# Expert rows read by a transposing DMA instead of a plain DMA and PE transposes

## The chip, the cores and the metric

The kernel runs on one core of a Trainium2 chip. A core has a matrix engine (PE, with its weight loads listed apart as PEld), a vector engine (DVE), a scalar engine (ACT), a general engine (POOL) and a queue engine (SP) that here only issues DMAs. Each engine works through its own queue in order and waits on semaphores that the others raise. DMAs are issued from the queues of SP and POOL and are moved by the core's 16 DMA engines. On-chip memory is SBUF (128 partitions) and PSUM, into which PE writes. The metric is the device time of one execution in microseconds; less is better.

## The reference

The program is blockwise causal attention followed by a mixture of experts with a noisy top-2 router. Cut to what matters:

```python
# attention: batch 8, 8 heads, 576 positions, head size 64; masked by blocks of 64 positions
attn = softmax(scale * q @ k.T, mask) @ v
x = attn.transpose(0, 2, 1, 3).reshape(4608, 512)        # N tokens, D = 512

# router: two experts of eight for each token
noisy = x @ w_gate + log1p(exp(x @ w_noise)) * noise
top2, top2_w = two largest of noisy, softmax over these two

# experts: D = 512 -> F = 1024 -> 512
for e in range(8):
    for k in range(2):
        mask = top2[:, k] == e
        h = np.maximum(x[mask] @ w1[e], 0.0)
        out[mask] += top2_w[mask, k, None] * (h @ w2[e])
```

## The kernel before

The kernel works in bfloat16 with accumulation in float32. The 4608 tokens are cut into four groups of two batch entries (g = 0 to 3, nine tiles of 128 tokens each) and two halves (half 0 is groups 0 and 1, half 1 is groups 2 and 3).

**Attention and router, for each group (L202 to L366).** q and k are loaded and transposed on PE, scores go through PE (L233) and ACT's exponential (L237), PE multiplies by v (L261, L275), and DVE normalizes into the tile `xr` (L279), one row of 512 numbers for each token. `xr` has two buffers, so groups 1 and 3 share one. The router transposes `xr` on PE, computes logits (L292), and DVE picks the two experts of each token and its place among the rows of each expert (L301 to L352); the counts come from two small matmuls `pp` (L328, L329). POOL then scatters each row of `xr` with 18 indirect DMAs for each group (L357) into a DRAM bucket, `xd[half]`, in which each expert has CAP = 640 rows.

**Experts, for each half and each of the eight experts (the loop over `seq`, from L430).** Experts are counted 0 to 15 here; 0 to 7 are the eight of half 0. `load_x` (L378) reads the 640 rows of one expert from the bucket into the tile `xg`, five blocks of 128 rows with a row in each partition, by one DMA on SP's queue; it depends on all scatters of that half. `xg` has three buffers, and the program asks for the load of expert i + 2 ahead of the work of expert i. `expert` (L386) then turns the rows into `xgT`, in which the partition is the place in d and the row is along the free axis: for each of four blocks of d, five PE transposes (L392) into one PSUM tile and one copy by DVE (L393). The first layer `hp` (L399) takes 64 matmuls of 128x128 by 320 columns; ACT applies the rectifier into `hsb` (L402), eight times for an expert. The second layer `yp` (L407) takes 40 matmuls of 512 columns, eight to a block of 128 rows; DVE casts each block into `ysb` (L410), and SP stores it to a second DRAM bucket `yd` (L411). `hp` and `yp` have two PSUM buffers each.

**Combine, once for each half (`combine`, L413 to L428).** For each of 18 tiles of tokens POOL gathers the two result rows of each token from `yd` with two indirect DMAs (L419), DVE weights and adds them (L424, L425), and SP stores the output (L428). The combine of half 0 comes in the program after expert 7 and ahead of expert 8, that of half 1 at the end.

**What sets the order.** The queues of the engines are in the order that the framework's scheduler chose when it built the program, which need not be that of the text: loads and transposes stand ahead of work that waits. Dependencies between instructions become semaphore waits. The pools of the expert part (from L368, opened when those of the attention part have closed) take SBUF that the attention part used; the first writer of a tile waits for whoever used that memory last. The pools open in the order weights `wL`, `xgp` (3 buffers of 5,120 B in each partition), `xgtp` (2 of 5,120 B), `hp` (2 of 10,240 B), `yp` (6 of 1,024 B), `fin`.

**Weights.** Those of experts 0 and 1 of each half (the same eight sets serve both halves) are loaded during the last attention group, the others by POOL-issued DMAs after it (L113 to L118, called at L433).

A branch for buckets that overflow (from L452) is compiled in and isn't taken with these inputs.

Of the kernel before, what the change touches and what calls it, by code (L numbers as in the profile page):

```python
# [9 lines left out]
BF16 = mybir.dt.bfloat16  # L10
# [9 lines left out]
def kernel(  # L20
# [12 lines left out]
    nc = tc.nc  # L33

    B, H, S, D = q.shape
    N, Dm = out.shape
# [3 lines left out]
    P = 128  # L40
    DB = Dm // P
# [6 lines left out]
    CAP = 640  # L48
    CT = CAP // P
# [9 lines left out]
    xd = [nc.dram_tensor(f"xd{i}", (XR, Dm), BF16, kind="Internal").ap() for i in range(NH)]  # L59
# [16 lines left out]
    ident = consts.tile([P, P], BF16)  # L76
# [50 lines left out]
    with tc.tile_pool(name="raw", bufs=2) as raw_pool, \  # L127
# [61 lines left out]
        for i in range(NH):  # L189
            zr = OVB // P  # L190
            nc.sync.dma_start(
                out=xd[i][0:OVB, :].rearrange("(p a) d -> p (a d)", p=P).rearrange("p (a c) -> p a c", c=2048),
                in_=zero.unsqueeze(1).to_broadcast([P, zr * Dm // 2048, 2048]))
# [8 lines left out]
        for g in range(NG):  # L202
            half = g // 2
# [15 lines left out]
            for st in range(H // SET):  # L219
# [33 lines left out]
                for idx in range(TG):  # L253
                    av = av_ps.tile([P, SET, D + 1], F32, tag="av")
                    for hh in range(SET):
                        h = st * SET + hh
                        if idx < 8:
                            hf, ib = divmod(idx, 4)
                            for jt in range(ib + 1):
                                c = EO[jt] + (ib - jt) * P  # L260
# [3 lines left out]
                        else:  # L264
                            for jt in range(5):
                                for hf in range(2):
                                    sl = slice(64 * hf, 64 * hf + 64)
                                    if jt < 4:
                                        c = EO[jt] + (4 - jt) * P
# [15 lines left out]
            for idx in range(TG):  # L285
                tp = tr_ps.tile([P, DB, P], BF16, tag="tr")
# [80 lines left out]

    with tc.tile_pool(name="wL", bufs=1) as wL, \  # L368
         tc.tile_pool(name="xgp", bufs=3) as xg_pool, \
         tc.tile_pool(name="xgtp", bufs=2) as xgt_pool, \  # L370
         tc.tile_pool(name="hp", bufs=2) as h_pool, \
         tc.tile_pool(name="yp", bufs=6) as y_pool, \
         tc.tile_pool(name="fin", bufs=4) as fin, \
# [2 lines left out]
         tc.tile_pool(name="ft_ps", bufs=2, space=PSUM) as ft_ps:  # L376

        def load_x(half, e):  # L378
            xg = xg_pool.tile([P, CT, Dm], BF16, tag="xg")
            ins = nc.sync.dma_start(out=xg, in_=xd[half][e * CAP:(e + 1) * CAP, :]  # L380
                                    .rearrange("(c p) d -> p c d", p=P))
            for nm in scat[half]:
                tc.add_manual_dep(ins.ins, nm, SYNC_DEP, reason="rows landed")
            return xg

        def expert(half, e, xg):  # L386
            w1sb, w2sb = wload[e]
            xgT = xgt_pool.tile([P, DB, CAP], BF16, tag="xgT")
            for db in range(DB):
                tp = ft_ps.tile([P, CAP], BF16, tag="ft")  # L390
                for c in range(CT):
                    nc.tensor.transpose(tp[:, c * P:(c + 1) * P], xg[:, c, db * P:(db + 1) * P], ident)  # L392
                nc.vector.tensor_copy(xgT[:, db, :], tp)  # L393
            hsb = h_pool.tile([P, FB, CAP], BF16, tag="hsb")
            for fb in range(FB):
                hp = hp_ps.tile([P, 2, 512], F32, tag="hp")
                for db in range(DB):
                    for n in range(2):
                        nc.tensor.matmul(out=hp[:, n, 0:NW], lhsT=w1sb[:, db, fb * P:(fb + 1) * P],  # L399
                                         rhs=xgT[:, db, n * NW:(n + 1) * NW],  # L400
                                         start=(db == 0), stop=(db == DB - 1))
                nc.scalar.activation(out=hsb[:, fb, :].rearrange("p (n w) -> p n w", n=2),  # L402
                                     in_=hp[:, :, 0:NW], func=AF.Relu)
            for c in range(CT):
                yp = yp_ps.tile([P, Dm], F32, tag="yp")
                for fb in range(FB):
                    nc.tensor.matmul(out=yp, lhsT=hsb[:, fb, c * P:(c + 1) * P], rhs=w2sb[:, fb, :],  # L407
                                     start=(fb == 0), stop=(fb == FB - 1))
                ysb = y_pool.tile([P, Dm], BF16, tag="ysb")
                nc.vector.tensor_copy(ysb, yp)  # L410
                nc.sync.dma_start(out=yd[half][e * CAP + c * P:e * CAP + (c + 1) * P, :], in_=ysb)  # L411
# [120 lines left out]
```

## Time and profile before

| | us |
|---|---|
| median of 3 runs | 726.08 |
| lowest and highest | 724.75 to 729.91 |
| the profiled execution | 728.31 |
| its span (first to last instruction) | 726.50 |
| PE busy in the span | 472.7 |
| DVE busy | 253.3 |
| ACT busy | 187.3 |
| POOL busy | 218.7 |

The profile is one execution, recorded by the hardware. Times are microseconds from the start of the span unless marked ns. A row of the timeline gives the start, the length, the engine, the line of the kernel, the operation, what it writes and reads, the number of instructions merged in the row and, in brackets, how long the engine had been idle before it and what ended that. A row of the chain of waits gives start, length and the work; the chain is followed back from the last instruction to whatever released each step. A group row gives the line, the engine, the operation, the shapes and the count, then busy time and mean ns, then the idle time ahead of it by releaser. In the table of stretches each row has the busy time and the count of instructions of each engine within one stretch, the TensorE clock that was granted as a share of full speed, the share of time for which the DMA engines were busy, and what they moved.

### The profile page before, as it was taken

The page shows a single profiled execution, that of the slowest core. Times are in us where ns is not written, and L with a number is a line of the kernel's source. Part 1 is how long each engine was busy: PE and PEld are TensorE (multiplying, and loading weights), DVE is VectorE, ACT ScalarE, POOL GpSimd, SP SyncE. Part 2 cuts the span into 40 slices and gives each one's busy share as a digit, 9 for nine tenths or more (in the row PEclk, how much of TensorE's full clock was granted, in tenths as well). Part 3 has the DMA queues.
Part 4 walks back from the last instruction along what each step waited for, and adds up shares of the span by engine and source line. Part 5 has one row for each costly group of instructions (what it writes and reads, how often), then busy time and mean ns, then how long its engine had stood idle before and what let it go on. Part 6 is the DMA issues. An engine that isn't in the chain of part 4 may idle for free.

```text
span 726.5 us, 10418 instructions
## 1 busy us (share of the span) xinstructions
PE 472.7 (65%) x4264; PEld 292.6 (40%) x4264; DVE 253.3 (35%) x591; ACT 187.3 (26%) x245; POOL 218.7 (30%) x244
## 2 busy tenths in 40 slices
PE   2087788361786284039999999964179999996000
PEld 1045446130563163025555555541055555553000
DVE  3054946150474155002222222235332222221443
ACT  0084480160415130013322222230033322221000
POOL 5126625777004413370000000077600000001773
PEclk9988866555566566559999999995589999999555
DMA  9999999492001209969942212256432221111564
GB/s 207 343 231 169 181 195 177 142 124 101 1 2 60 73 15 260 210 133 221 226 125 73 71 55 59 72 176 200 150 105 73 73 73 37 37 37 46 177 192 146
DMA packets 102902, 91.62 MB, mean 126 GB/s; under 512 B 49088, under 2 KB 86976, under 8 KB 102848
## 3 DMA queue, kind: packets, MB, share of 16 engines
q0 software_dynamic: 67744, 49.84, 45.8%
q1 hardware_dynamic: 35104, 41.05, 17.7%
q8 instruction: 35, 0.57, 0.3%
q14 instruction: 19, 0.16, 0.1%
HBM read 81.97 MB, written 39.85 MB: 168 GB/s over the span
## 4 chain that ended last, share of the span: by engine, by line
PE 50%; issue 12%; DMA 9%; another core or an unknown queue 9%; POOL 7%; DVE 7%; ACT 6%; POOLq 0%; DVEq 0%; ACTq 0%; SPq 0%
PE hp L399 18%; PE yp L407 18%; ACT esc L237 6%; POOL yg L419 4%; DMA kr<-in_k_dram 4%; PE av L261 4%; DMA vt<-in_v_dram 3%; PE sc L233 2%; PE av L275 2%; POOL xd L357 2%; PE tp L392 2%; PE tp L166 2%; DVE ysb L410 1%; PE tp L288 1%
## 5 line engine op out<-in xcount | busy, mean ns | idle before, releaser
L399 PE MATMUL hp<-xgT,w 128*128 128x320 bf16 x1024 | 149.9, 305 | 33.6 <-ACT hsb L402 33.6
L419 POOL DMA_INDIRECT yg<-yd,gslots x72 | 75.6, 1050 | 317.6 <-PE hp L399 149.4
L402 ACT ACTIVATE hsb<-hp 128x640 bf16<-128x640 f32 x128 | 89.9, 703 | 288.7 <-PE hp L399 246.6
L407 PE MATMUL yp<-w,hsb 128*128 128x512 bf16 x640 | 146.4, 388 | 17.8 <-DVE ysb L410 14.8
L399 PEld LDWEIGHTS <-w 128*128 128x128 bf16 x1024 | 101.5, 100 | 74.8 <-issue 34.0
L410 DVE CAST ysb<-yp 128x512 bf16<-128x512 f32 x80 | 55.3, 691 | 212.3 <-PE yp L407 203.3
L237 ACT ACTIVATE esc<-sc 128x1024 bf16<-128x1024 f32 x96 | 91.5, 1036 | 127.8 <-PE sc L233 72.2
L407 PEld LDWEIGHTS <-hsb 128*128 128x128 bf16 x640 | 63.5, 99 | 94.5 <-issue 24.5
L357 POOL DMA_INDIRECT xd<-xr,slots x72 | 71.0, 986 | 92.8 <-DVE slots L352 46.9
L233 PE MATMUL sc<-qT,kT 64*128 64x512 bf16 (+4 forms) x320 | 52.8, 376 | 29.4 <-ACT esc L237 27.4
L261 PE MATMUL av<-vt,esc 128*128 128x65 bf16 x640 | 42.6, 234 | 38.5 <-DVE xr L279 29.7
L261 PEld LDWEIGHTS <-esc 128*128 128x128 bf16 x640 | 34.4, 123 | 52.9 <-DVE xr L279 35.1
L155 POOL DMA_DIRECT2D vt<-in_v_dram x40 | 33.7, 867 | 53.6 <-DMA kr<-in_k_dram 14.2
L392 PE MATMUL tp<-ident,xg 128*128 128x128 bf16 x320 | 27.7, 233 | 28.5 <-DVE xgT L393 24.6
L393 DVE COPY xgT<-tp 128x640 bf16<-128x640 bf16 x64 | 29.0, 486 | 47.9 <-PE hp L399 44.8
L392 PEld LDWEIGHTS <-xg 128*128 128x128 bf16 x320 | 23.0, 105 | 35.8 <-DVE xgT L393 17.6
L278 DVE RECIPROCAL rden<-av 128x4 f32<-128x4 f32 x72 | 13.0, 182 | 68.1 <-remote 41.7
L166 PE MATMUL tp<-ident,qr 128*64 128x128 bf16 (+1 forms) x320 | 18.8, 274 | 27.2 <-DMA qr<-in_q_dram 14.8
L233 PEld LDWEIGHTS <-kT 64*128 64x128 bf16 x320 | 15.1, 102 | 51.5 <-issue 47.2
L172 DVE COPY qT<-tp 128x1024 bf16<-128x1024 bf16 (+1 forms) x20 | 22.3, 1117 | 33.8 <-PE tp L166 20.3
L425 DVE SCALAR_TENSOR_TENSOR acc<-yg,wts,acc 128x512 f32<-128x512 bf16 x36 | 26.5, 748 | 17.8 <-DMA yg<-yd,gslots 17.7
L424 DVE TENSOR_SCALAR acc<-yg,wts 128x512 f32<-128x512 bf16 x36 | 19.0, 529 | 35.8 <-DMA yg<-yd,gslots 31.1
(78 smaller groups left out, 278.9 us busy)
## 6 DMA issues: line engine op xcount, KB each, us to landing
w<-in_moe_w_dram POOLq DMA_DIRECT2D x16, 1024.0 KB
xd<-zero SPq DMA_DIRECT2D x2, 5120.0 KB
xg<-xd SPq DMA_DIRECT2D x16, 640.0 KB
yd<-ysb SPq DMA_DIRECT2D x80, 128.0 KB
out_dram<-acc SPq DMA_DIRECT2D x32, 256.0 KB
vt<-in_v_dram POOLq DMA_DIRECT2D x32, 128.0 KB
qr<-in_q_dram POOLq DMA_DIRECT2D x8, 384.0 KB
kr<-in_k_dram POOLq DMA_DIRECT2D x8, 384.0 KB
```

The source lines that it names most:

```text
L155: nc.gpsimd.dma_start(out=vb[p0:p0 + n, idx, :, 0:D], in_=v[b, :, s0:s0 + n, :].rearrange("h s d -> s h d"))
L166: nc.tensor.transpose(tp[64 * hf:64 * hf + 64, r * n:(r + 1) * n], raw[p0:p0 + n, src_t, r * 64:(r + 1) * 64], ident[p0:p0 + n, p0:p0 + n])
L233: nc.tensor.matmul(out=sc[:, hf, off:off + z - a], lhsT=kT[sl, c0 + jt * P:c0 + jt * P + P], rhs=qT[sl, c0 + a:c0 + z], start=True, stop=True)
L237: nc.scalar.activation(out=esc[:, hh, :, u * 512:(u + 1) * 512], in_=sc, func=AF.Exp, scale=scale)
L261: nc.tensor.matmul(out=av[:, hh, :], lhsT=esc[:, hh, hf, c:c + P], rhs=vb[:, 4 * hf + jt, h, :], start=(jt == 0), stop=(jt == ib))
L357: ins = nc.gpsimd.indirect_dma_start(out=xd[half], out_offset=bass.IndirectOffsetOnAxis(ap=slots[:, t0 + idx, i:i + 1], axis=0), in_=xr[:, ...
L392: nc.tensor.transpose(tp[:, c * P:(c + 1) * P], xg[:, c, db * P:(db + 1) * P], ident)
L399: nc.tensor.matmul(out=hp[:, n, 0:NW], lhsT=w1sb[:, db, fb * P:(fb + 1) * P], rhs=xgT[:, db, n * NW:(n + 1) * NW], start=(db == 0), stop=( ...
L402: nc.scalar.activation(out=hsb[:, fb, :].rearrange("p (n w) -> p n w", n=2), in_=hp[:, :, 0:NW], func=AF.Relu)
L407: nc.tensor.matmul(out=yp, lhsT=hsb[:, fb, c * P:(c + 1) * P], rhs=w2sb[:, fb, :], start=(fb == 0), stop=(fb == FB - 1))
L410: nc.vector.tensor_copy(ysb, yp)
L419: nc.gpsimd.indirect_dma_start(out=yg[:, i, :], out_offset=None, in_=yd[half], in_offset=bass.IndirectOffsetOnAxis(ap=gslots[:, t, i:i + 1 ...
```

## The change

The load of an expert's rows becomes a DMA that transposes 2-byte elements on its way from the bucket into SBUF, and writes the layout [d, row] that the first layer reads. The tile `xg` keeps its three buffers and its 5,120 B in each partition, with the shape of `xgT`. The transposes on PE, their PSUM tile and the copies by DVE are gone from `expert`, and so is the pool `xgtp`. The `ft` PSUM pool stays, for the overflow branch. The load is issued from the same queue, with the same dependencies on the scatters.

```diff
     with tc.tile_pool(name="wL", bufs=1) as wL, \
          tc.tile_pool(name="xgp", bufs=3) as xg_pool, \
-         tc.tile_pool(name="xgtp", bufs=2) as xgt_pool, \
          tc.tile_pool(name="hp", bufs=2) as h_pool, \
...
         def load_x(half, e):
-            xg = xg_pool.tile([P, CT, Dm], BF16, tag="xg")
-            ins = nc.sync.dma_start(out=xg, in_=xd[half][e * CAP:(e + 1) * CAP, :]
-                                    .rearrange("(c p) d -> p c d", p=P))
+            xg = xg_pool.tile([P, DB, CAP], BF16, tag="xg")
+            ins = nc.sync.dma_start_transpose(out=xg, in_=xd[half][e * CAP:(e + 1) * CAP, 0:Dm])
             for nm in scat[half]:
                 tc.add_manual_dep(ins.ins, nm, SYNC_DEP, reason="rows landed")
             return xg

-        def expert(half, e, xg):
+        def expert(half, e, xgT):
             w1sb, w2sb = wload[e]
-            xgT = xgt_pool.tile([P, DB, CAP], BF16, tag="xgT")
-            for db in range(DB):
-                tp = ft_ps.tile([P, CAP], BF16, tag="ft")
-                for c in range(CT):
-                    nc.tensor.transpose(tp[:, c * P:(c + 1) * P], xg[:, c, db * P:(db + 1) * P], ident)
-                nc.vector.tensor_copy(xgT[:, db, :], tp)
             hsb = h_pool.tile([P, FB, CAP], BF16, tag="hsb")
```

## The prediction

> **What bounds the kernel now.** I read three views: the table of stretches (busy time of each engine from one moment to the next), the chain of waits for the moments at which work ends, and the timeline for what each engine waited on. The stretches come first (columns: stretch, its length, busy us and instructions of PE, PEld, DVE, ACT and POOL, granted PE clock, DMA share, GB/s).
>
> ```profile
> span 726.5 us, 10418 instructions
> core 0: us, PE busy (x) PEld busy (x) DVE busy (x) ACT busy (x) POOL busy (x), PEclk, DMA share, GB/s
> 0.00:269.50 269.50, 157.12 (x2226) 103.66 (x2226) 118.67 (x338) 96.71 (x114) 115.24 (x142) 0.69 0.95 135
> 269.50:319.00 49.50, 11.47 (x122) 8.76 (x123) 11.56 (x45) 0.73 (x4) 22.77 (x24) 0.59 0.84 199
> 319.00:470.00 151.00, 147.12 (x931) 87.58 (x931) 37.21 (x64) 44.87 (x64) 5.06 (x7) 0.98 0.52 116
> 470.00:530.00 60.00, 25.26 (x133) 13.01 (x130) 26.93 (x47) 5.62 (x8) 38.30 (x36) 0.69 0.55 176
> 530.00:667.00 137.00, 131.71 (x858) 79.55 (x858) 36.23 (x64) 39.37 (x56) 0.00 (x0) 0.99 0.17 56
> 667.00:726.50 59.50, 0.00 (x0) 0.00 (x0) 22.66 (x36) 0.00 (x0) 37.28 (x36) 0.53 0.52 162
> ```
>
> Attention runs to 269.5 and the diff does not touch it. In the two stretches of expert work, 319 to 470 and 530 to 667, PE is busy 147.1 of 151 and 131.7 of 137 us at a clock of 0.98 and 0.99: PE sets the pace there. In 269.5 to 319 and 470 to 530 PE works 11.5 and 25.3 us and otherwise waits; there the question is for what. After 667 no PE work is left (the last gathers).
>
> One expert in steady state, from the chain (start, length, what), the timeline and the groups of the page:
>
> ```profile
> 384.13 8.65 PE yp L407 x40
> 392.60 0.72 PE L392 MATMUL tp<-ident,xg 128*128 128x128 bf16 x10
> 393.41 1.92 DVE L393 COPY xgT<-tp 128x640 bf16<-128x640 bf16 x4
> 393.94 0.44 PE L392 MATMUL tp<-ident,xg 128*128 128x128 bf16 x5 [0.62 <-DVE xgT L393]
> 394.80 8.62 PE hp L399 x63
> 403.42 8.65 PE yp L407 x40
> L392 PE MATMUL tp<-ident,xg 128*128 128x128 bf16 x320 | 27.7, 233 | 28.5 <-DVE xgT L393 24.6
> L393 DVE COPY xgT<-tp 128x640 bf16<-128x640 bf16 x64 | 29.0, 486 | 47.9 <-PE hp L399 44.8
> ```
>
> From one second layer (yp) to the next is 403.42 - 384.13 = 19.29 us. Of these 8.62 are hp and 8.65 yp; the other 2.02 us are the twenty transposes of x and PE's wait of 0.62 for the copies out of PSUM.
>
> The two stretches in which PE waits:
>
> ```profile
> 269.72 12.45 SPq L380 DMA_DIRECT2D xg<-xd  x5
> 274.34 1.09 PEld L392 LDWEIGHTS <-xg 128*128 128x128 bf16 x11 [0.70 <-DMA xg<-xd]
> 275.10 0.49 DVE L393 COPY xgT<-tp 128x640 bf16<-128x640 bf16 x1 [0.53 <-PE tp L392]
> 279.44 0.19 PE L328 MATMUL pp<-m,ones_mat 128*128 128x72 bf16 x1
> 280.26 0.48 DVE L393 COPY xgT<-tp 128x640 bf16<-128x640 bf16 x1
> 284.90 0.98 PEld L392 LDWEIGHTS <-xg 128*128 128x128 bf16 x10 [3.29 <-DMA xg<-xd]
> 284.20 1.05 POOL L357 DMA_INDIRECT xd<-xr,slots  x1 [10.62 <-DVE cmax L446]
> 303.54 0.98 POOL L357 DMA_INDIRECT xd<-xr,slots  x1 [4.08 <-DMA w<-in_moe_w_dram]
> 318.97 1.30 ACT L402 ACTIVATE hsb<-hp 128x640 bf16<-128x640 f32 x2 [39.55 <-DMA xd<-xr,slots]
> 319.73 9.60 PE L399 MATMUL hp<-xgT,w 128*128 128x320 bf16 x48 [33.58 <-ACT hsb L402]
> 346.65 8.63 PE yp L407 x40
> 364.84 8.65 PE yp L407 x40
> 461.28 8.65 PE yp L407 x40
> 473.45 1.07 POOL L419 DMA_INDIRECT yg<-yd,gslots  x1 [149.39 <-PE hp L399]
> 510.20 3.47 PE L407 MATMUL yp<-w,hsb 128*128 128x512 bf16 x8 [1.84 <-issue]
> 521.90 1.01 POOL L419 DMA_INDIRECT yg<-yd,gslots  x1 [0.30 <-issue]
> 524.91 0.69 DVE L410 CAST ysb<-yp 128x512 bf16<-128x512 f32 x1 [9.03 <-remote]
> 529.95 0.88 DVE L393 COPY xgT<-tp 128x640 bf16<-128x640 bf16 x2
> 530.49 1.25 PE L392 MATMUL tp<-ident,xg 128*128 128x128 bf16 x10 [16.82 <-DVE xgT L393]
> 531.74 9.83 PE hp L399 x64
> 541.57 8.65 PE yp L407 x40
> 657.30 8.65 PE yp L407 x40
> ```
>
> At the start expert 0's x has landed by 274.34, yet ACT's first write to hsb waits 39.55 us, until 318.97, for the scatter of the last group (xd<-xr). The scatter writes DRAM; hsb waits because it lies where xr lay, and the scatter reads xr until then. In the combine PE is done with expert 8 at 510.20 + 3.47 = 513.67 and idles 16.82 us: expert 9's transposes need PSUM that DVE frees by the xgT copies, and those stand behind the whole combine in DVE's queue (529.95).
>
> **The change, part by part.**
>
> Removed: 320 transposes and weight loads on PE, 64 copies on DVE (27.7 and 29.0 us busy in the groups above). On the path each steady expert loses its 2.02 us and falls to 8.62 + 8.65 = 17.27. The cover under it: ACT needs 0.70 us (44.87 / 64 in the stretch from 319) per hp group of 1.08 and DVE 0.69 (the cast at 524.91) per yp group of 1.73, so neither becomes the bound. Experts 3 to 7 and 10 to 15 give 11 x 2.02 = 22.2 us. Expert 2, half of whose transposes ran early, ends at 364.84 + 8.65 = 373.49, 18.21 after expert 1 (346.65 + 8.63 = 355.28); it gives 0.94. Experts 0 and 1 were transposed before 319: nothing from PE.
>
> Moved: the pool of xgT (two buffers of 4 x 640 x 2 = 5,120 B a partition) goes, so hp, y and fin, opened behind it, lie 10,240 B lower, if pools lie in the order in which they open. One hsb buffer is 8 x 640 x 2 = 10,240 B, exactly the two xgT buffers. So the first hsb comes to lie where xgT lay, and DVE wrote both xgT buffers by 275.10 and 280.26, forty us before the scatter ended. The second hsb takes the place of the first and waits for 318.97 as that did; ysb (6 x 1,024 B) takes the place of the second. Expert 0 can then do all of hp and, with two PSUM banks, two of its five yp groups before 319; the fill of two hp groups of expert 1, which PE did for expert 0 before, stays. From 319.73 on are left 24 yp matmuls (24 x 8.65 / 40 = 5.19), 48 hp of expert 1 (48 x 8.62 / 64 = 6.47), its yp (8.65), and the slow clock after the idle time: the 48 hp after the stall took 9.60 instead of 6.47, so 3.13. Expert 1 ends at 319.73 + 5.19 + 6.47 + 8.65 + 3.13 = 343.17 instead of 355.28: 12.1 us. Bounds: nothing (rival 2) to 15 with a warm clock.
>
> Through expert 7: 343.17 + 6 x 17.27 = 446.79 against 461.28 + 8.65 = 469.93, a gain of 23.1. Weights do not hold it: DMA is busy for 0.52 of the 151 us from 319, 78.5 us; were all of that, and at the front, the weights of experts 4 to 7, they would land at 339, 358, 378 and 397, and these experts now start at 378, 395, 412 and 430.
>
> The combine: DVE passed its end 529.95 - 469.93 = 60.0 us after expert 7, paced by POOL, whose 36 gathers go from 473.45 to 521.90, 48.45 / 35 = 1.38 each. Nothing of that changes, so DVE is through at 446.79 + 60.0 = 506.8. But hp of expert 9 needs no DVE now: PE goes on right after expert 8 (40.2 us after the first gather, so about 490.5) and has hp and two yp groups done by the time DVE is free. Left are one cast (0.69), 24 yp matmuls (5.19) and a cold clock: between 1.2 and 3.1 us (hp of expert 9 took 9.83 in the chain; of expert 0, above); I take 2. Expert 9 ends at 514.7 instead of 541.57 + 8.65 = 550.2: 35.5, of which 12.4 come from this stretch.
>
> ```profile
> L380 SPq DMA_DIRECT2D xg<-xd x16: 360/371/524, 269.7 to 590.8; - x16
> q0 software_dynamic: 67744, 49.84, 45.8%
> ```
>
> Added: sixteen transposing loads on SP instead of plain ones, 655,360 B each. No row shows one. Nearest below: the plain load, from issue at 269.72 to 274.34, 4.6 us. Above: by packets. The software queue's took 0.458 x 726.5 x 16 / 67,744 = 78.6 ns each on an engine; if every 256 B run of a row (one block of 128 elements) is a packet, a load has 2,560, or 12.6 us over 16 engines. I take about 5, near the plain row, since the bytes and the queue are the same. Every load is asked for well ahead: its buffer frees when hp of the expert three before is done, that is 8.6 us later than now, with two experts and more (over 34.5 us) to land in. So both 4.6 and 12.6 cost nothing there.
>
> The Trainium skill speaks against this: "VectorE: DVE Perf Modes", section "The three transpose paths", gives 1309 ns for a 128x128 block by the DMA crossbar, so twenty blocks would be an estimated 26.2 us, and the sum would come out near 766. Its page "DMA: Bandwidth & Descriptors", section "Latency and other measured facts", gives 261 GB/s for a transposing DMA, an estimated 2.5 us, and leaves the sum as it is. No run here shows either; the first of the two is a case of rival 1 and within its chance.
>
> New waits and queues: a load now waits on SP for hp of its buffer's last expert, and behind it stand that expert's five yd stores. If SP is held for the whole load (a plain one holds it 0.37 us) and that is 12.6, the last store of expert 7 leaves 8.6 + 12.6 - 17.3 = 3.9 late and delays the combine by so much; at 5 nothing. POOL's queue keeps its order. PE has the two pp matmuls of the router (279.44) behind the first expert work; if x of expert 0 lands 8 us later, they and the scatter start that much later, but the scatters start at 284.20, one in 1.35, and the eighth was held for weight loads until 303.54, 9.9 us after it could have gone, so that is covered too.
>
> Sum: 23.1 + 12.4 + 6 x 2.02 (experts 10 to 15) = 47.6. The profiled execution took 728.31 (span 726.5 and 1.8 around it), 2.2 above the median of 726.08. From the median: 678.5; I say 679.
>
> **Rivals.**
> Rival 1, slower: the transposing loads set the pace. They run one behind another from 269.72, so the last lands at 269.72 + 16T and its expert ends 17.27 later; before it ended at 657.30 + 8.65 = 665.95. The point that decides is T = 23.7 us. If the load is cut into 128 B pieces, 5,120 packets of 78.6 ns over 16 engines make T = 25.2: end 690, time 750. Against it: three plain loads had landed by 284.90, beside weight loads (DMA share 0.84).
> Rival 2: nothing is pulled ahead of 319 (hsb still waits for the scatter, or PE's order does not let expert 0 through). Then the first half gives 0.94 + 5 x 2.02 = 11.0 instead of 23.1: 691. The place of hsb is worked out, not seen.
> Rival 3: expert 9 does not get ahead, because DVE's queue has the casts of expert 8 too late in the combine (one stood at 524.91 after 9.03 us that no engine explains). Then that stretch gives 2.0 instead of 12.4: 689.
> That T lies near 23.7 and all cancels is the case of no change.
>
> **How the numbers follow.** The forecast 0.66, rival 2 0.12, rival 3 0.12, no change 0.04, rival 1 0.06. A measurement of this kernel tells about 1% from nothing. Faster by more: 0.66 + 0.12 + 0.12 = 0.90; within: 0.04; slower: 0.06. The range goes up to 700 (rivals 2 and 3 together give 25.2: 701) and down to 668 (the 9.03 us stall gone as well, 670, and less lost to a cold clock).
>
> **What would show it.** Right: hp and yp alternate without a gap every 17.3 us; ACT's first hsb write lies before 290; experts 0 and 1 have 112 matmuls left after 319 instead of 192; hp of expert 9 starts before DVE ends the combine; PE no longer waits for xgT. Wrong: PE waiting for DMA xg<-xd (rival 1), a first hsb write still at 319 (rival 2), PE idle between experts 8 and 9 until the combine's end (rival 3), the scatter ending later than 319, or yd stores held back behind a load on SP.

## The result, and the profile after

The changed kernel takes 703.86 us (median of 4 runs, 701.40 to 708.35) against 727.52 (724.75 to 729.91) for the kernel before on the same chip: a ratio of 0.968, with a 95% interval of 0.962 to 0.975. It is faster, by 23.7 us, half of the 47 forecast, and its time lies just above the range of 668 to 700. Its profiled execution took 701.40 with a span of 699.5; it was the fastest of the four, so its span lies 27.0 us below that of the profile before, more than the 23.7 between the medians. Executions that took over 1.5% longer than the fastest of their kernel (one each of after_again, c5_lay_w and the kernel before in session 2) are left out of the times and ratios below.

The stretches of the changed kernel, cut where the work changes (columns as before):

```profile
core 0: us, PE busy (x) PEld busy (x) DVE busy (x) ACT busy (x) POOL busy (x), PEclk, DMA share, GB/s
0.00:269.00 269.00, 155.64 (x2229) 102.38 (x2230) 119.11 (x338) 96.93 (x114) 115.24 (x142) 0.71 0.93 135
269.00:313.40 44.40, 7.14 (x70) 4.49 (x71) 8.15 (x33) 0.70 (x3) 21.78 (x23) 0.57 0.97 169
313.40:379.40 66.00, 55.61 (x303) 31.05 (x303) 10.79 (x19) 16.77 (x24) 6.06 (x8) 0.90 1.16 201
379.40:465.30 85.90, 85.90 (x516) 50.35 (x515) 16.63 (x25) 28.12 (x40) 0.00 (x0) 1.00 0.32 76
465.30:533.00 67.70, 40.37 (x210) 22.04 (x208) 28.40 (x46) 11.14 (x16) 37.47 (x36) 0.75 0.64 179
533.00:637.00 104.00, 104.00 (x625) 60.88 (x623) 20.75 (x30) 33.74 (x48) 0.00 (x0) 1.00 0.21 58
637.00:699.50 62.50, 0.07 (x1) 0.00 (x0) 23.76 (x37) 0.00 (x0) 38.26 (x36) 0.53 0.51 156
```

From 379.4 on, in the stretches of experts alone, PE is busy 85.9 of 85.9 and 104 of 104 us: there the change does what it says. Between 313.4 and 379.4, where experts 0 to 2 run, PE stands still for more than 10 of 66 us. That is new.

The chain of waits of the changed kernel has the steady experts, and the place where they are not steady:

```profile
314.17 9.26 PE hp L391 x48
323.43 8.29 PE yp L399 x39
331.72 20.26 DMA yd<-ysb
352.85 5.65 PE yp L399 x16
364.94 9.28 DMA yd<-ysb
375.09 3.61 PE yp L399 x16
430.68 8.69 PE hp L391 x64
439.38 8.63 PE yp L399 x40
448.01 8.69 PE hp L391 x64
```

A steady expert takes 448.01 - 430.68 = 17.33 us, for 17.27 forecast. But twice the chain leaves PE for a store of `ysb`, for 20.26 and 9.28 us. Without that, expert 2 would have ended at 323.43 + 8.65 + 2 x 17.33 = 366.7; it ends at 375.09 + 3.61 = 378.70. So 12.0 us are lost here.

The timeline of the changed kernel shows why those stores are late, and what the start of the experts waits for (SP's rows are the time for which its queue was taken by the DMA instruction, not the transfer; the row of 62.31 us holds the first four loads and the gaps between them):

```profile
269.06 62.31 SPq L379 DMA_TRANSPOSE xg<-xd  x4
281.01 3.63 PE L391 MATMUL hp<-xg,w 128*128 128x320 bf16 x13 [8.29 <-DMA xg<-xd]
288.11 1.05 POOL L357 DMA_INDIRECT xd<-xr,slots  x1 [16.07 <-DVE slots L352]
310.91 0.98 POOL L357 DMA_INDIRECT xd<-xr,slots  x1 [0.30 <-issue]
313.42 1.30 ACT L394 ACTIVATE hsb<-hp 128x640 bf16<-128x640 f32 x2 [37.42 <-DMA xd<-xr,slots]
323.46 7.91 SPq L379 DMA_TRANSPOSE xg<-xd  x1
331.72 9.96 SPq L403 DMA_DIRECT2D yd<-ysb  x5
341.79 23.06 SPq L379 DMA_TRANSPOSE xg<-xd  x1
352.11 0.69 DVE L402 CAST ysb<-yp 128x512 bf16<-128x512 f32 x1 [8.89 <-DMA yd<-ysb]
364.94 4.38 SPq L403 DMA_DIRECT2D yd<-ysb  x5
369.41 6.41 SPq L379 DMA_TRANSPOSE xg<-xd  x1
374.34 1.29 DVE L402 CAST ysb<-yp 128x512 bf16<-128x512 f32 x2 [4.69 <-DMA yd<-ysb]
559.16 2.71 SPq L379 DMA_TRANSPOSE xg<-xd  x1
```

The reader is to see two things. First, SP is taken for 7.91, 23.06 and 6.41 us by the loads of x for experts 3, 4 and 5, and in between it issues the stores of a whole expert in one go: they have queued behind the load. The six `ysb` buffers run out, DVE's cast waits for a store (8.89 and 4.69 us), and PE waits for DVE. The queue is not all of it: the store whose buffer the first of these waits is for was issued at 331.72, 5.8 us after its cast was done, and landed only 20.26 us later (the chain's row). Late in the program, when the weights have long been loaded, the same load takes SP 2.71 us. Second, ACT's first write to `hsb` still waits for the scatter (37.42 us), at 313.42 instead of 318.97: nothing was pulled ahead of the scatter's end, but that end came 5.5 us earlier, 0.7 of it because the attention ended that much sooner in this execution (269.06 against 269.72).

Where the 27.0 us between the two spans (726.5 and 699.5) come from, by the ends of experts 7, 9 and 15 in the two traces:

| stretch | before | after | gain | forecast |
|---|---|---|---|---|
| up to the end of expert 7 | 469.93 | 465.33 | 4.6 | 23.1 |
| from there to the end of expert 9 (combine) | 80.29 | 67.78 | 12.5 | 12.4 |
| experts 10 to 15 | 115.73 | 103.97 | 11.8 | 12.1 |
| after the last expert | 60.55 | 62.42 | -1.9 | 0 |

The miss lies almost wholly in the first row. Of its 23.1, 11.0 were the transposes of experts 2 to 7, and 12.1 the work pulled ahead. Measured: 11.0, nothing pulled ahead, 12.0 lost in experts 0 to 2, and 5.5 from the earlier end of attention and scatter: 11.0 - 12.0 + 5.5 = 4.5.

### The profile page after: what moved, and what is told of

Same layout as the page of the kernel before. It is cut to its first block, busy times and chain, and to the rows that moved or that the text cites. A ratio compares the mean times of both kernels' runs of the same rounds, so it can differ in the third digit from the quotient of the medians.

```text
span 699.5 us, 9743 instructions
## 1 busy us (share of the span) xinstructions
PE 448.7 (64%) x3944; PEld 271.2 (39%) x3944; DVE 227.6 (33%) x527; ACT 187.4 (27%) x245; POOL 218.8 (31%) x244
## 2 busy tenths in 40 slices
DMA packets 133875, 91.58 MB, mean 131 GB/s; under 512 B 90304, under 2 KB 117952, under 8 KB 133824
## 4 chain that ended last, share of the span: by engine, by line
PE 48%; DMA 13%; another core or an unknown queue 12%; issue 10%; ACT 7%; POOL 5%; DVE 3%; POOLq 1%; SPq 0%; DVEq 0%; ACTq 0%
PE hp L391 18%; PE yp L399 17%; DMA vt<-in_v_dram 7%; ACT esc L237 7%; DMA yd<-ysb 5%; PE av L261 4%; PE sc L233 2%; PE tp L166 2%; POOL yg L411 2%; PE av L275 2%; POOL xd L357 2%; PE tp L288 1%; DMA yg<-yd,gslots 1%; DVE xr L279 1%
## 5 line engine op out<-in xcount | busy, mean ns | idle before, releaser
L391 PE MATMUL hp<-xg,w 128*128 128x320 bf16 x1024 | 149.9, 309 | 50.4 <-ACT hsb L394 42.1
L391 PEld LDWEIGHTS <-w 128*128 128x128 bf16 x1024 | 103.0, 101 | 96.6 <-issue 51.0
L233 PE MATMUL sc<-qT,kT 64*128 64x512 bf16 (+4 forms) x320 | 52.4, 375 | 38.1 <-ACT esc L237 32.7
L261 PE MATMUL av<-vt,esc 128*128 128x65 bf16 x640 | 42.1, 233 | 34.6 <-DVE xr L279 15.3
L279 DVE TENSOR_TENSOR xr<-av,rden 128x256 bf16<-128x256 f32 x72 | 28.5, 415 | 1.1
L166 PEld LDWEIGHTS <-qr 128*64 128x64 bf16 (+1 forms) x320 | 13.9, 139 | 31.9 <-DMA qr<-in_q_dram 24.1
L172 DVE COPY kT<-tp 128x1024 bf16<-128x1024 bf16 (+1 forms) x20 | 22.5, 1124 | 10.7 <-PE tp L166 5.5
```

The lines of the kernel that those rows point to most:

```text
L166: nc.tensor.transpose(tp[64 * hf:64 * hf + 64, r * n:(r + 1) * n], raw[p0:p0 + n, src_t, r * 64:(r + 1) * 64], ident[p0:p0 + n, p0:p0 + n])
L172: nc.vector.tensor_copy(dv, pv)
L233: nc.tensor.matmul(out=sc[:, hf, off:off + z - a], lhsT=kT[sl, c0 + jt * P:c0 + jt * P + P], rhs=qT[sl, c0 + a:c0 + z], start=True, stop=True)
L261: nc.tensor.matmul(out=av[:, hh, :], lhsT=esc[:, hh, hf, c:c + P], rhs=vb[:, 4 * hf + jt, h, :], start=(jt == 0), stop=(jt == ib))
L279: nc.vector.tensor_tensor(out=xr[:, idx, st * SET * D:(st + 1) * SET * D].rearrange("p (h d) -> p h d", h=SET), in0=av[:, :, 0:D], in1=rde ...
```

## The experiments

Two lengths are read from each trace. A is the time from the issue of x of expert 0 (the end of the attention) to the first `hsb` write. B is the time from the last cast of expert 0 to the last cast of expert 3, by DVE's timeline; three steady experts are 3 x 17.33 = 51.98. Times are compared only among runs of one session, since the kernel before itself took 669.20 in the first session, 730.75 in the second and 726.68 in the third; A and B don't depend on the attention, where that difference lies mostly.

| kernel | us | ratio to before (95%) | A | B |
|---|---|---|---|---|
| before | 727.52 | 1 | 49.3 | - |
| changed | 703.86 | 0.968 (0.962 to 0.975) | 44.4 | 63.95 |
| *session 1* (before 669.20) | | | | |
| e1_plain | 624.23 | 0.933 (0.931 to 0.935) | 39.7 | 51.98 |
| e2_ysb16 | 630.63 | 0.941 (0.938 to 0.944) | 43.8 | 51.98 |
| e3_hp_split | 626.15 | 0.939 (0.933 to 0.945) | 14.2 | 62.14 |
| e4_act_stores | 641.03 | 0.958 (0.956 to 0.960) | 43.2 | 62.66 |
| *session 2* (before 730.75) | | | | |
| after_again | 706.42 | 0.968 (0.964 to 0.972) | - | - |
| c2_both | 680.25 | 0.931 (0.926 to 0.935) | 15.6 | 49.67 |
| c3_layout | 673.08 | 0.919 (0.913 to 0.924) | 14.8 | 52.74 |
| e5_no_w | 683.31 | 0.934 (0.930 to 0.937) | 38.1 | 51.98 |
| *session 3* (before 726.68) | | | | |
| e6_w_behind | 702.84 | 0.967 (0.963 to 0.972) | 38.1 | 70.38 |
| e7_pp | 703.66 | 0.967 (0.960 to 0.974) | 42.6 | 69.20 |
| c5_lay_w | 665.64 | 0.913 (0.907 to 0.919) | 9.0 | 53.42 |
| c6_lay_pp | 669.91 | 0.920 (0.916 to 0.925) | 14.3 | 61.94 |

Each edit below is against the changed kernel. The times in the first four expectations were meant for a session like that of the first comparison; session 1 was a quicker one, and the changed kernel itself was not run in it, so what an edit brought there is read from A and B and from the differences among the four.

### Is it the transposing load that holds SP? (e1_plain)

```diff
-            ins = nc.sync.dma_start_transpose(out=xg, in_=xd[half][e * CAP:(e + 1) * CAP, 0:Dm])
+            ins = nc.sync.dma_start(out=xg.rearrange("p b c -> p (b c)").rearrange("p (c d) -> p c d", c=CT),
+                                    in_=xd[half][e * CAP:(e + 1) * CAP, :].rearrange("(c p) d -> p c d", p=P))
```

> The x load is a plain load of the rows into the same bytes, so the transposition is left out altogether. Theory A: it is the transposing load itself that holds SP while the weights come in (7.9 us for x of expert 3, 23.1 for x of expert 4), and yd's stores stand behind it. Then SP issues each load at once, no DVE cast of experts 0 to 2 waits for a store, these three end within 53 us of the first hsb write (65.3 in the changed kernel), and x of expert 0 lands some 7 us sooner, so that the last scatter can end earlier by up to 8. The time is 12 to 20 us below the changed kernel: 684 to 692. Rival theory, that yd's stores themselves are slowed by the weights' traffic, whatever the form of the x load: the DVE waits stay, and the time is 696 to 704. Under both the steady experts keep 17.3 us.

This kernel leaves the transposition out. The group row of its x loads (least, median and greatest ns on the queue), and, from the timeline, its first `hsb` write:

```profile
L379 SPq DMA_DIRECT2D xg<-xd x16: 359/371/524, 215.3 to 500.2; - x16
```

```profile
254.99 1.30 ACT L395 ACTIVATE hsb<-hp 128x640 bf16<-128x640 f32 x2 [32.79 <-DMA xd<-xr,slots]
```

No load holds SP for more than 0.524 us, B is three steady experts, and A is 4.1 us shorter than in e2_ysb16 of the same session. The 12.0 of B and these 4.1 make 16: theory A's band of 12 to 20. The stores of experts 0 to 3 land at most 10.5 us after their issue here, beside the same weights, against the 20.26 of the changed kernel. The plain load of the same bytes brings no stall, so it is the form of the load that matters, not the traffic alone.

### Is the stall in experts 0 to 2 a shortage of buffers behind SP? (e2_ysb16)

```diff
-         tc.tile_pool(name="yp", bufs=6) as y_pool, \
+         tc.tile_pool(name="yp", bufs=16) as y_pool, \
```

> 16 ysb buffers in place of 6. Theory A: the stores still leave late behind the transposing loads, but three experts' stores have 16 tiles to wait in, so no DVE cast waits for a store; experts 0 to 2 lose no 12 us, and the time is 12 below the changed kernel, about 690 to 693. Rival theory, that the 12 us in experts 0 to 2 have another cause (weights of expert 2 or 3 late, or x of expert 3 or 4): 701 to 705, with PE waiting for a DMA of xg or w in place of DVE. SBUF behind this pool moves up by 10,240 B, which by both theories costs nothing.

Rows of its timeline:

```profile
288.53 23.27 SPq L379 DMA_TRANSPOSE xg<-xd  x1
306.51 0.69 DVE L402 CAST ysb<-yp 128x512 bf16<-128x512 f32 x1 [9.73 <-PE yp L399]
312.31 3.22 SPq L403 DMA_DIRECT2D yd<-ysb  x5
```

SP is held for 23.27 us as before and the stores still wait for it, but now DVE's cast waits only for PE, and B falls from 63.95 to 51.98. The 12.0 us were the wait of six buffers for late stores, as theory A has it.

### Would the stores be free on ACT's queue? (e4_act_stores)

```diff
-                nc.sync.dma_start(out=yd[half][e * CAP + c * P:e * CAP + (c + 1) * P, :], in_=ysb)
+                nc.scalar.dma_start(out=yd[half][e * CAP + c * P:e * CAP + (c + 1) * P, :], in_=ysb)
```

> yd's stores are issued by ACT in place of SP, so that no transposing load stands ahead of them. Theory A: no DVE cast of experts 0 to 2 waits for a store, 12 us go, 690 to 694 (ACT's own queue now holds the stores between its Relu writes, which may cost some of that: an issue waits for the cast). Rival theory, that the stores are slow because of the weights' traffic and not because of SP: the waits stay, 701 to 706.

From its timeline, the load of x for expert 4 on SP, the stores of expert 1 on ACT's queue and the rectifier behind them:

```profile
286.08 22.73 SPq L379 DMA_TRANSPOSE xg<-xd  x1
288.54 0.33 ACTq L403 DMA_DIRECT2D yd<-ysb  x1
297.94 1.29 ACTq L403 DMA_DIRECT2D yd<-ysb  x3
299.82 1.30 ACT L394 ACTIVATE hsb<-hp 128x640 bf16<-128x640 f32 x2 [13.02 <-issue]
```

This expectation failed in the time, though no cast waits for a store any more. While SP is in its load (from 286.08), ACT issues one store at 288.54 and gets the next away only at 297.94, though DVE had begun the casts for it and its follower at 289.55 and 291.27; its own next instruction, the rectifier that PE waits for, comes 13.02 us late. B is 62.66, 1.3 below the changed kernel, and the run is 10.4 us above e2_ysb16 of the same session. So theory A was too narrow: what the transposing load holds is not SP's queue only; stores issued by ACT stand still for part of it too, and there they take ACT's computation along. That it is the load and not the weights' traffic that stops them is argued only: in e1_plain, beside the same weights, each store of experts 0 to 3 took SP 0.32 to 0.33 us, but stores on ACT beside a plain load were not run. The Trainium skill's page "DMA: Bandwidth & Descriptors", section "Issuing engines are not separate DMA queues", says that DMAs of all issuing engines run on the same DMA engines and that spreading them saves only issue time. This run agrees and adds that the issue time is not always saved either (9.4 us between two stores).

### Is it the weights' traffic that stretches the load? (e5_no_w)

```diff
+        wdum = wL.tile([P, (E - 2) * (DB * F + FB * Dm)], BF16, name="wdum")
+        nc.vector.memset(wdum[:, 0:1], 0.0)
         for e in range(2, E):
-            load_w(wL, e)
+            wload[e] = wload[e % 2]
```

> The weights of experts 2 to 7 are not loaded at all (these experts compute with those of experts 0 and 1), so no such traffic runs under the x loads. Theory A': it is the traffic of the weights that stretches the transposing load and holds SP. Then all loads from expert 2 on take SP 2.4 to 3.0 us, as in the quiet stretches, no cast waits for a store, experts 0 to 2 end within 53 us of the first hsb write, and x of expert 0 is sooner; the time is 12 to 22 below the changed kernel. Rival theory: the long holds come of something else at that place (the waits for an xg buffer, the scatters, the stores themselves): the holds of 8 and 23 us stay, and the time is the changed kernel's within 3 us.

The group row of its x loads:

```profile
L379 SPq DMA_TRANSPOSE xg<-xd x16: 2499/2781/4131, 274.4 to 561.2; - x16
```

This kernel leaves out the weights of experts 2 to 7. Sixteen transposing loads and none above 4.13 us on SP (that one among the gathers of the combine), B three steady experts, A 38.1. Without the weights the load is as harmless as the prediction took it; with them it holds SP up to 23 us. Theory A' stands. The time, 23.1 below after_again, is 1 more than the band's upper end; B and A account for 12.0 + 6.3 of it, and the rest was not traced.

### What holds the first hsb? (e3_hp_split)

```diff
-         tc.tile_pool(name="hp", bufs=2) as h_pool, \
+         tc.tile_pool(name="hpa", bufs=1) as h_pool, \
+         tc.tile_pool(name="hpb", bufs=1) as h_pool2, \
...
-            hsb = h_pool.tile([P, FB, CAP], BF16, tag="hsb")
+            hsb = (h_pool, h_pool2)[e % 2].tile([P, FB, CAP], BF16, tag="hsb")
```

> The hsb pool is cut in two pools of one buffer each, at the same addresses; the first lies over bytes that only the exponentials of the attention held, the second reaches into the rows that the scatters read. Theory B: the wait for released memory goes by whole pools, so the first hsb, in a pool of its own, waits for the attention alone. Then the first hsb write comes at 282 to 290 (313 in the changed kernel), expert 0's hp and first two yp groups run before the last scatter ends, and the time is about 12 us lower, 688 to 694 (a little more or less as the stores of expert 0 shift against the loads of x). Rival theory, that the wait goes by bytes or that something else than memory holds the first hsb (the scatters' semaphores reach ACT for another reason): the first write stays at 313 and the time at 701 to 705.

Its timeline has the first `hsb` write, the first casts and the longest wait for a store:

```profile
227.19 0.70 ACT L395 ACTIVATE hsb<-hp 128x640 bf16<-128x640 f32 x1 [10.06 <-PE hp L392]
256.69 1.29 DVE L403 CAST ysb<-yp 128x512 bf16<-128x512 f32 x2 [25.01 <-DMA xd<-xr,slots]
301.71 0.69 DVE L403 CAST ysb<-yp 128x512 bf16<-128x512 f32 x1 [10.77 <-DMA yd<-ysb]
```

At the same addresses, the first write to `hsb` comes 14.2 us after x of expert 0 is issued instead of 44, and waits for PE, not for the scatter. So theory B stands: in the changed kernel it waited for the scatter because the *pool* of `hsb`, its second buffer, overlaps the pool of `xr`; the first buffer shares no byte with it. Expert 0 ends 52.5 us after the issue of its x (63.4 in e2_ysb16), 10.8 sooner, and expert 1 some 13 sooner (67.5 against 80.7). The casts wait for the scatter still, since the `ysb` pool lies over `xr`, and the 12 us stall behind SP stays almost whole (B 62.14, the wait of 10.77 at 301.71).

### Both at once (after_again, c2_both)

c2_both joins the diffs of e2_ysb16 and e3_hp_split; after_again is the changed kernel.

> The changed kernel itself, on the chip of the runs beside it, so that each of them has it to be compared with. By the stage times of the first four experiments (attention, scatter and combine of these runs, with the changed kernel's 12 us stall in experts 0 to 2): 640 to 648, and a ratio to the kernel before near 0.96. If the stores issued by ACT brought nothing, its time is that run's, 641; if they brought the 12 us expected of them, 653.

> The first hsb in a pool of its own and 16 ysb buffers together. Theory: the two losses are independent, one before the scatter's end (about 14 us in the expert-0 end of the split alone) and one in the stores of experts 0 to 2 (12 us), so both go: first hsb write near 227, no DVE wait for a store, 610 to 617, some 26 below the changed kernel. Rival theory: with the experts 14 us earlier the x loads, still held by the weights' traffic (up to 23 us each, more than an expert's 17.3), set the pace, PE waits for xg, and the time stays at 622 to 628.

The first `hsb` write in c2_both's timeline:

```profile
285.20 0.70 ACT L395 ACTIVATE hsb<-hp 128x640 bf16<-128x640 f32 x1 [11.50 <-PE hp L392]
```

The session was another than the first four kernels', so the 640 to 648 expected of after_again failed, and its time says nothing about e4_act_stores; its ratio, 0.968, repeats the first result. c2_both is 26.2 us below it, where "some 26" were expected. Its expected times, worked out from session 1, mean 52 to 59 below the kernel before, by the rival 41 to 47; the measured 50.5 lies between the two bands. No DVE cast waits for a store, PE waits for xg once behind expert 0 (3.71 us), and B is even below three steady experts, because the first matmuls of expert 1 ran during the scatter. The two losses add up but for a few us: counted from the issue of x of expert 0 by DVE's timeline, expert 3 ends 12.4 us sooner than in the changed kernel with 16 buffers, 13.0 sooner with the split pool and 22.8 with both. They are the size of the miss: with both undone the ratio is 0.931 (0.926 to 0.935), against 679 / 726.08 = 0.935 forecast.

### Why the scatter ended 5.5 us earlier (e6_w_behind, e7_pp)

In the kernel before, four weight loads stand ahead of the last 18 scatters on POOL's queue; in the changed one three do (the scheduler put the fourth behind them). Two edits try that:

```diff
         for e in range(2, E):
-            load_w(wL, e)
+            for ins in load_w(wL, e):
+                tc.add_manual_dep(ins.ins, scat[NH - 1][-1], ORD, reason="behind the scatters")
```

> The changed kernel with all weight loads of experts 2 to 7 behind the last scatter on POOL's queue (three of them stand ahead of the scatters before). Theory C: the weights that run beside x of expert 0 and the scatters are what delays them: from the issue of x of expert 0 to the first hsb write it was 49.3 us with four loads ahead (the kernel before), 44.4 with three (the changed one), 38.1 with none at all. Then it is 37 to 40 here, x of expert 0 lands in about 5 us instead of 12, and 4 to 7 us go; the stall in experts 0 to 2 (12 us) stays or grows by a few, as all the weights now come under them. Ratio to the kernel before 0.955 to 0.964. Rival theory: that the last scatter ends earlier in the changed kernel has nothing to do with POOL's order (it is the x load's form, or POOL's own pace): 43 to 46 us, ratio 0.966 to 0.972.

```diff
-            nc.tensor.matmul(out=pp[:, 1, :], lhsT=prem, rhs=mf, start=True, stop=True)
+            ppi = nc.tensor.matmul(out=pp[:, 1, :], lhsT=prem, rhs=mf, start=True, stop=True)
...
+                        if (half, e, fb, db, n) == (0, 0, 0, 0, 0):
+                            tc.add_manual_dep(mm.ins, ppi.ins.name, ORD, reason="routing first")
```

> The changed kernel with the two routing matmuls ahead of expert 0's matmuls on PE, so that the scatters start without waiting for x of expert 0 (some 8 us sooner). By theory C the scatters then start beside the three weight loads, as in the kernel before, where 18 of them took 34.8 us from the first issue to the first hsb write against 25.3 in the changed kernel: most of the 8 us is lost again, the first hsb write comes 39 to 46 us after x of expert 0 was issued (44.4 in the changed kernel), ratio 0.962 to 0.970. Rival theory, that POOL's own pace (1.29 us a scatter) sets their time: 35 to 37 us, and 8 us go, ratio 0.955 to 0.960.

From the timeline of e6_w_behind the first `hsb` write and two long holds of SP after it, and from that of e7_pp the first and last scatter:

```profile
308.81 1.30 ACT L397 ACTIVATE hsb<-hp 128x640 bf16<-128x640 f32 x2 [31.23 <-DMA xd<-xr,slots]
337.64 21.85 SPq L380 DMA_TRANSPOSE xg<-xd  x1
365.39 18.36 SPq L380 DMA_TRANSPOSE xg<-xd  x1
```

```profile
282.34 1.05 POOL L357 DMA_INDIRECT xd<-xr,slots  x1 [7.78 <-DVE slots L352]
311.65 0.98 POOL L357 DMA_INDIRECT xd<-xr,slots  x1 [0.30 <-issue]
```

With no weights ahead (e6_w_behind), A is 38.1, as without any weights at all: theory C. But the ratio stays at 0.967, above the 0.955 to 0.964 expected: B grows by 6.4 to 70.38, because the weights now come wholly under experts 0 to 2 and hold SP for 21.85 and 18.36 us. What is gained ahead is lost behind. In e7_pp the scatters start 10.8 us after the issue of x of expert 0 (19.1 in the changed kernel) but take 311.65 - 282.34 = 29.3 us for the 18 instead of 310.91 - 288.11 = 22.8: beside the weight loads they run slower, as theory C expected (A 42.6, ratio 0.967); B grew there too, to 69.20, and why is not shown. POOL's rows say where the time goes: in the kernel before three of the 18 scatters wait for weight loads, 11.2 us together, in e7_pp two, 7.9 us, in the changed kernel none. So the earlier scatter of the changed kernel is a matter of the weights ahead of it and of when it starts, and not a merit of the transposing load: e1_plain, with three weight loads ahead and a plain load of x, has an A of 39.7. A changed kernel with four loads ahead was not run.

### A layout that goes further (c3_layout, c5_lay_w, c6_lay_pp)

```diff
-         tc.tile_pool(name="hp", bufs=2) as h_pool, \
-         tc.tile_pool(name="yp", bufs=6) as y_pool, \
+         tc.tile_pool(name="hpa", bufs=1) as h_pool, \
          tc.tile_pool(name="fin", bufs=4) as fin, \
+         tc.tile_pool(name="pad", bufs=1) as pad_pool, \
+         tc.tile_pool(name="hpb", bufs=1) as h_pool2, \
+         tc.tile_pool(name="yp", bufs=15) as y_pool, \
...
-        cmax = fin.tile([P, 2], F32, tag="cmax")
+        cmax = keep.tile([P, 2], F32)
```

`pad` is a filler, `keep` an older pool elsewhere, and `expert` picks its `hsb` pool as in e3_hp_split. c5_lay_w adds the edit of e6_w_behind to it, c6_lay_pp that of e7_pp.

> No hsb or ysb buffer lies over the rows that the scatters read: the combine's buffers do, and both hsb pools and 15 ysb buffers are free once the routing is done; the overflow flag's small tiles are elsewhere too. Theory: experts 0 and 1 run as soon as x of expert 0 has landed (about 225), expert 1 ends near 264 (296.8 with 16 ysb buffers alone), the scatter's end no longer holds anything of the experts, and the time is 596 to 603. Rival theory: the x loads set the pace as in the entry before, since experts 2 to 5 now fall wholly within the weights' traffic, or a weight load is late: PE waits for xg or w, and the time is 608 to 625.

> The layout of the entry c3_layout with the weight loads behind the scatters as well. Theory: x of expert 0 lands some 7 us sooner, the routing matmuls behind its first 13 too, and with them the whole run of scatters and the experts, whose DVE and ACT work stood still until the scatters had all been issued: 5 to 9 us below c3_layout, ratio 0.905 to 0.913. Rival theory: the weights of experts 2 and 3 are late then, PE waits for a DMA of w, ratio 0.917 to 0.93.

> The layout of the entry c3_layout with the routing matmuls ahead of expert 0's. Theory: as the work of DVE and ACT in experts 0 and 1 stands still until the scatters have all been issued, their end sets the experts' start, and it moves as far as in e7_pp: 0 to 5 us below c3_layout, ratio 0.910 to 0.919. Rival theory: the standstill of DVE and ACT has nothing to do with the scatters, and the time is that of c3_layout or above.

The timeline of c3_layout while the scatters go out:

```profile
303.12 0.69 DVE L404 CAST ysb<-yp 128x512 bf16<-128x512 f32 x1 [2.20 <-PE yp L401]
309.73 0.69 DVE L404 CAST ysb<-yp 128x512 bf16<-128x512 f32 x1 [5.93 <-remote]
318.91 0.69 DVE L404 CAST ysb<-yp 128x512 bf16<-128x512 f32 x1 [8.48 <-remote]
319.05 1.30 ACT L396 ACTIVATE hsb<-hp 128x640 bf16<-128x640 f32 x2 [21.80 <-remote]
315.30 0.98 POOL L357 DMA_INDIRECT xd<-xr,slots  x1 [0.30 <-issue]
```

The times of c3_layout's expectation, too, were worked out from session 1: 66 to 73 us below the kernel before by the theory, 44 to 61 by the rival. The measured 57.7 is in the rival's band, but not for the rival's reason: PE waits for no x behind that of expert 0 and for no weight. No `hsb` write and no cast waits for the scatter any more, and still DVE and ACT stand still, released by something that the profile can't name ("remote"), until POOL has issued its last scatter (315.30). So expert 1 ends 64.4 us after the issue of x of expert 0, 5.9 sooner than in c2_both (70.2).

c5_lay_w ends at a ratio of 0.913, the upper edge of the 0.905 to 0.913 expected, with an interval up to 0.919; c6_lay_pp ends at 0.920, just past its band's 0.919, where the rival theory had it. The intervals overlap, and the traces show the same gain ahead of the combine in both: expert 7 ends 162.8 and 163.0 us after the issue of x of expert 0, 168.3 in c3_layout. From there to the end of expert 9 it takes 71.3 and 70.4 us, 67.2 in c3_layout. So the times don't settle what the scatters do to DVE and ACT. In c6_lay_pp DVE makes the five casts of expert 0 with some 1.03 us of rest between them (295.39 to 302.30) amid the scatters (282.21 to 311.75), so the scatters alone don't stop it. c5_lay_w has the largest gain of the study: 8.7% below the kernel before (8.1 to 9.3).

## Why the prediction was half right

**The steady expert: right.** 17.33 against 17.27, no wait for the copies, and neither ACT nor DVE became the bound. Experts 10 to 15 gave 11.8 of 12.1.

**The pull-ahead: failed, at the step "the first hsb comes to lie where xgT lay".** The place was worked out rightly, and the wait was not: it goes by whole pools, not by buffers (e3_hp_split). That the row of before fitted both readings was the trap: in that kernel, `xgT`'s pool overlapped no byte of `xr`'s and was free early, while `hsb`'s did. The prediction's rival 2, at a chance of 0.12, is what happened. The work itself would have fitted: with the pool split it comes, worth some 13 us at the end of expert 1 in e3_hp_split (against e2_ysb16) for 12.1 forecast.

**The transposing load "costs nothing": failed, at the step "at 5 nothing".** The landing was judged well only where the weights don't run. In the three kernels of session 1 with transposing loads the profile gives the time from issue to landing: the median is 5.0 to 6.8 us, near the 5 taken, and the longest 29.4 to 34.6, far above the bound of 12.6. The row of e2_ysb16 (least, median, greatest), whose longest is the load of x for expert 4, issued at 288.53:

```profile
DMA to landing us min/median/max: 4.8/5.0/30.8
```

x of expert 0 was there 12.0 us after its issue beside the weights (269.06 to 281.01), and 6.4 with the weights behind (e6_w_behind). The count of packets also came out: the changed profile has 41,216 more packets under 512 B than before (90,304 and 49,088), 2,576 for each load against 2,560 worked out.

```profile
DMA packets 133875, 91.58 MB, mean 131 GB/s; under 512 B 90304, under 2 KB 117952, under 8 KB 133824
```

What was mis-sized is the time on SP, which the prediction took to be the landing time at the most, and its price, for which it looked only at the last store of expert 7 (3.9 us at the most). Stores held back behind a load on SP were among its own signs of being wrong. The hold was up to 23.06 us, and it fell on experts 0 to 2, whose stores have six buffers; 12.0 us were lost. The prediction had itself put most of the weights' traffic behind 319, where loads 3, 4 and 5 are issued (in the stretches after, the DMA share is 1.16 there and 0.32 behind), and had still priced the load there at about 5 us, as if it ran alone.

Of the Trainium skill's two figures, 261 GB/s ("DMA: Bandwidth & Descriptors", "Latency and other measured facts"), an estimated 2.5 us for a load, comes near the time on SP once the weights are loaded, 2.4 to 3.0 us, but the load lands in 5.0 us at the median (e2_ysb16), twice the estimate. The 1309 ns for a block ("VectorE: DVE Perf Modes", "The three transpose paths"), an estimated 26.2, does not: twenty blocks took 2.71 at 559.16. The long holds come near it only by the weights' traffic (e5_no_w).

**"POOL's queue keeps its order": wrong, in the kernel's favour.** One weight load moved behind the scatters, and the first `hsb` write came 4.9 us sooner after the issue of x of expert 0 (A 44.4 for 49.3); e6_w_behind shows that this order matters, though not that the one load is all of the 4.9.

**The combine: the size right, the way only in part.** 12.5 against 12.4. Expert 9 did begin ahead of the combine's end, but only by two groups of `hp`; ACT wrote the first of them at 514.12 only, 12.7 us after PE had both ready (499.49 + 1.93 = 501.42), while POOL's gathers went from 468.88 to 519.54 (timeline of the changed kernel):

```profile
499.49 1.93 PE L391 MATMUL hp<-xg,w 128*128 128x320 bf16 x13
514.12 1.30 ACT L394 ACTIVATE hsb<-hp 128x640 bf16<-128x640 f32 x2 [39.35 <-remote]
514.88 9.60 PE L391 MATMUL hp<-xg,w 128*128 128x320 bf16 x48 [13.45 <-ACT hsb L394]
```

The forecast had all 64 `hp` and two `yp` groups done by the time DVE was free; measured, 48 `hp` and all of `yp` were left, but from 514.9 on, ten us before the moment forecast (465.33 + 60.0 = 525.3). That the two errors cancel is chance. Rival 3 did not happen, though PE still waited 13.88 us for a cast of expert 8 (until 491.77).

With the two failed steps undone, c2_both ends near where the forecast put the changed kernel, in part by luck: expert 7 ends some 174 us after the issue of x of expert 0, where the forecast has 446.79 - 269.72 = 177.1, and from there to the end of expert 9 it takes 71.4 us for 514.7 - 446.79 = 67.9.

## What to carry to other kernels

When a DMA changes its form, price the time for which it holds the queue that issues it beside the traffic of *that* moment, list what stands behind it on that queue, and count how many buffers those have; more buffers cured it here, another issuing engine did not. Memory that a change frees or moves helps only if the dependency on it is as fine as the arithmetic: look at what the first writer waits for, pool by pool. And where a change deletes instructions, look at what the scheduler then does with the other queues.

## What the runs showed of the hardware that was not expected

A transposing DMA of 655,360 B took its issuing queue 2.4 to 3.0 us in the changed kernel where neither weights nor gathers moved, and up to 23.70 us (c6_lay_pp) beside weight loads from POOL, while the plain load of the same bytes took 0.36 to 0.52 us in both places (e1_plain). During one such load 9.4 us passed between two stores issued by ACT, the second of which had its cast done 7.7 us before (e4_act_stores).

During POOL's runs of scatters and gathers idle times of DVE and ACT of up to 40.61 us (e6_w_behind) ended with no releaser that the profile names, in the kernels of the second and third session and in both kernels compared here. Part of each is time in which the engine had nothing to do. In the first session no such wait is in any of the four traces, and there the kernel before took 669.20 instead of 727.52. What the standstill is stays open; it was not tried. In c3_layout and c5_lay_w it is the wait that ends last ahead of expert 1 (21.80 us of ACT in c3_layout, for which PE waits 11.88).
